# Turning q and k by VectorE 32x32 transposes, with four-tile scores, a list schedule and shared PSUM banks

## The chip, the cores and the metric

The kernel runs on one core of one Trainium2 chip. The metric is device time in microseconds (us) of one execution. A run over 1.5% above the fastest of the same kernel is called slow and takes no part in a ratio. TensorE is called PE, its weight loads PEld, VectorE DVE, ScalarE ACT, GpSimd POOL, as in the profile.

## The reference, cut to what matters

Attention with a window of 128 keys and four sink keys, in 4 batches of 8 heads, followed by an MLP mixer on each batch.

```python
B, H, S, D = 4, 8, 768, 64            # q, k, v = randn * 0.1; n_sink 4, window 128
keep = is_sink | ((rel >= 0) & (rel < window))
a = softmax(where(keep, q @ k.T / 8, -1e9))
x = (a @ v) -> [4, 768, 512]
h = relu(x.T @ w_tok1) @ w_tok2       # w_tok1 [768, 256]
u = x + h.T
out = u + relu(u @ w_ch1) @ w_ch2     # w_ch1 [512, 1536], out float32
```

The two channel matmuls are called ch1 and ch2 below, the token matmuls tok1 and tok2. In the profile ch1 writes the tile `ps_v`, ch2 `ps_w`, tok1 `ps_h`, tok2 `ps_u`, the scores `ps_s`, probabilities times v `ps_o`. A group is four heads, so there are eight groups, g0 to g7, two for each batch.

## The kernel before

q and k come with token in the partition, and the score matmuls of this kernel read them with the head dimension there. Heads go in pairs: six PE transposes turn 2 heads x 768 tokens of q or k into PSUM, a VectorE copy takes the result out to bf16, and a score matmul contracts over 64 rows, two heads side by side.

```python
def load_qk(eng, src, dst, G, lo, hi):
    return eng.dma_start(out=dst[:, lo:hi].rearrange("p h t d -> p h (t d)"),
        in_=src[G.b, G.h0 + lo:G.h0 + hi].rearrange("h (p t) d -> p h (t d)", t=NT))
# ... (cut)
def tr(j, which):                       # j: pair of heads, which: q or k
    src = G.qb if which == 0 else G.kb
    ps = ps_ms.tile([P, NT, P], BF16, name="ps_tr", tag="ms")
    for t in range(NT):                 # NT = 6
        nc.tensor.transpose(ps[:, t], src[:, j, t].rearrange("p i d -> p (i d)"), ident)
    dst = att.tile([P, S], BF16, name="qT" if which == 0 else "kT")
    (by_act if g == 0 and j == 0 and which else by_dve)(
        dst.rearrange("d (p t) -> d p t", t=NT), ps.rearrange("d t p -> d p t"))
# ... (cut) scores of one pair:
    for kt, w in kts:
        for i in range(2):
            nc.tensor.matmul(ps[:, i, at:at + w],
                G.kT[j][ds(64 * i, 64), ts(kt, P)], G.qT[j][ds(64 * i, 64), ds(kt * P, w)], ...)
```

The copy out writes its destination without gaps and reads PSUM with a step. The order of instructions is made by hand: the attention of the next batch is spread between the mixer's matmuls by fractions. PSUM has two two-bank score tiles, two banks for the mixer (`mx`) and two for the rest (`ms`).

The softmax here doesn't subtract the row's maximum and nothing guards it: scores larger than these inputs give would overflow.

Of the kernel before, what the change touches and what calls it, by code (L numbers as in the profile page):

```python
# [12 lines left out]
ALU = mybir.AluOpType  # L13


@with_exitstack
def kernel(
# [13 lines left out]
    nc = tc.nc  # L31
# [12 lines left out]
    HS = S // 2  # L44
    D1 = D + 1
    scale = 1.0 / float(D) ** 0.5

    singles = ctx.enter_context(tc.tile_pool(name="singles", bufs=1))
    stage = ctx.enter_context(tc.tile_pool(name="stage", bufs=2))
    bfp = ctx.enter_context(tc.tile_pool(name="bfp", bufs=2))  # L50
    att = ctx.enter_context(tc.tile_pool(name="att", bufs=3))
    ptp = ctx.enter_context(tc.tile_pool(name="ptp", bufs=4))
    small = ctx.enter_context(tc.tile_pool(name="small", bufs=4))
    xpool = ctx.enter_context(tc.tile_pool(name="xpool", bufs=2))
    mix = ctx.enter_context(tc.tile_pool(name="mix", bufs=2))
    osb = ctx.enter_context(tc.tile_pool(name="osb", bufs=4))
    ps_sc = ctx.enter_context(tc.tile_pool(name="ps_sc", bufs=2, space=bass.MemoryType.PSUM))
    ps_mx = ctx.enter_context(tc.tile_pool(name="ps_mx", bufs=2, space=bass.MemoryType.PSUM))
    ps_ms = ctx.enter_context(tc.tile_pool(name="ps_ms", bufs=2, space=bass.MemoryType.PSUM))

    ident = singles.tile([P, P], BF16, name="ident")
    mask0 = singles.tile([P, 2, 2, P], BF16, name="mask0")
    mneg = singles.tile([P, 2, 2, 2, P], BF16, name="mneg")
    warm = singles.tile([P, 512], BF16, name="warm")
    ks = [[singles.tile([P, P], BF16, name=f"ks{a}{j}") for j in range(2)] for a in range(2)]
    vs_f = singles.tile([4 * GH, NG, GH, D1], FP32, name="vs_f")
    vsink = singles.tile([P, NG, GH, D1], BF16, name="vsink")

# [5 lines left out]
    SYNC = mybir.DependencyInfo(mybir.DependencyClass.Sync, mybir.DependencyReason.DATA)  # L74

    def after(dma, *others):
        for o in others:
            tc.add_manual_dep(dma.ins, o.ins.name, SYNC, reason="order of loads")
        return dma
# [4 lines left out]
    def tiles(g):  # L84
        G = Group()
        G.b, G.h0 = g // GB, GH * (g % GB)
        G.q32 = stage.tile([P, GH, NT, D], FP32, name="q32")
        G.k32 = stage.tile([P, GH, NT, D], FP32, name="k32")
        G.qb = bfp.tile([P, 2, NT, 2, D], BF16, name="qb")
        G.kb = bfp.tile([P, 2, NT, 2, D], BF16, name="kb")  # L90
        G.v32 = stage.tile([P, GH, NT, D], FP32, name="v32")
        G.va = bfp.tile([P, GH, NT, D1], BF16, name="va")
        G.qT, G.kT, G.pT = [None, None], [None, None], [None, None]
        return G


    def load_qk(eng, src, dst, G, lo, hi):
        return eng.dma_start(
            out=dst[:, lo:hi].rearrange("p h t d -> p h (t d)"),
            in_=src[G.b, G.h0 + lo:G.h0 + hi].rearrange("h (p t) d -> p h (t d)", t=NT))  # L100

    def load_q(G, lo, hi, eng=nc.sync):
        return load_qk(eng, q, G.q32, G, lo, hi)

    def load_k(G, lo, hi, eng=nc.sync):
        return load_qk(eng, k, G.k32, G, lo, hi)

    def cast(G, j, which, copy):
        src, dst = ((G.q32, G.qb), (G.k32, G.kb))[which]
        copy(dst[:, j].rearrange("p t i d -> p i t d"), src[:, 2 * j:2 * j + 2])  # L110

    def by_dve(o, i):
        nc.vector.tensor_copy(out=o, in_=i)  # L113

    def by_pool(o, i):
        nc.gpsimd.tensor_copy(out=o, in_=i)

    def by_act(o, i):
        nc.scalar.activation(o, i, AF.Copy)

    def load_v(G):
        return nc.sync.dma_start(out=G.v32.rearrange("p h t d -> p (h t) d"),
                                 in_=v[G.b, G.h0:G.h0 + GH].rearrange("h (t p) d -> p (h t) d", p=P))

    def load_sinks():
        for h in range(GH):
            nc.sync.dma_start(
                out=vs_f[4 * h:4 * h + 4, :, h, 0:D],
                in_=v.rearrange("b (a h) s d -> h s (b a) d", h=GH)[h, 0:4])

    def load_tok():
        nc.gpsimd.dma_start(out=w_tok1, in_=moe_w_tok1.rearrange("(t p) n -> p t n", p=P))
        nc.gpsimd.dma_start(out=w_tok2, in_=moe_w_tok2.rearrange("(t p) n -> p t n", p=P))

    def load_ch1(i):
        hf = DCH // 2
        return nc.gpsimd.dma_start(out=w_ch1[:, :, ts(i, hf)],
                            in_=moe_w_ch1.rearrange("(t p) n -> p t n", p=P)[:, :, ts(i, hf)])

    def load_ch2(i):  # L140
        hf = NF // 2
        nc.gpsimd.dma_start(out=w_ch2[:, ts(i, hf)],
                            in_=moe_w_ch2.rearrange("(t p) n -> p t n", p=P)[:, ts(i, hf)])

    def build_masks():

        z = mneg.rearrange("p m x c q -> p (m x) c q")
        nc.gpsimd.affine_select(
            out=z[:, :, 0], in_=z[:, :, 0], compare_op=ALU.is_ge,
            fill=-30000.0, base=0, pattern=[[0, 4], [1, P]], channel_multiplier=-1)  # L150
        nc.gpsimd.affine_select(
            out=z[:, :, 1], in_=z[:, :, 1], compare_op=ALU.is_ge,
            fill=-30000.0, base=-1, pattern=[[0, 4], [-1, P]], channel_multiplier=1)
        nc.vector.memset(mneg[0:4, 0, 0], 0.0)

    def build_mask0():
        nc.vector.memset(mask0, 1.0)
        nc.gpsimd.affine_select(
            out=mask0[:, :, 0], in_=mask0[:, :, 0], compare_op=ALU.is_ge,
            fill=0.0, base=0, pattern=[[0, 2], [1, P]], channel_multiplier=-1)  # L160
        nc.gpsimd.affine_select(
            out=mask0[:, :, 1], in_=mask0[:, :, 1], compare_op=ALU.is_ge,
            fill=0.0, base=-1, pattern=[[0, 2], [-1, P]], channel_multiplier=1)
        nc.vector.memset(mask0[0:4], 1.0)

    def build_sinks():

        one = vs_f[:, :, :, D]
        nc.gpsimd.memset(one, 1.0)
        nc.gpsimd.affine_select(  # L170
            out=one, in_=one, compare_op=ALU.is_ge, fill=0.0,
            base=0, pattern=[[0, NG], [-4, GH]], channel_multiplier=1)
        nc.gpsimd.affine_select(
            out=one, in_=one, compare_op=ALU.is_ge, fill=0.0,
            base=3, pattern=[[0, NG], [4, GH]], channel_multiplier=-1)

    def cast_sinks():
        nc.vector.tensor_copy(out=vsink[0:4 * GH], in_=vs_f)

    def cast_v(G):  # L180
        nc.gpsimd.memset(G.va[:, :, :, D:D1], 1.0)
        nc.gpsimd.tensor_copy(out=G.va[:, :, :, 0:D], in_=G.v32)


    def attention(g, G, x_b, first):
        c0 = GH * D * (g % GB)
        kz = ks[g % 2]

        def tr(j, which):
            src = G.qb if which == 0 else G.kb  # L190
            ps = ps_ms.tile([P, NT, P], BF16, name="ps_tr", tag="ms")
            for t in range(NT):
                nc.tensor.transpose(ps[:, t], src[:, j, t].rearrange("p i d -> p (i d)"), ident)  # L193
            dst = att.tile([P, S], BF16, name="qT" if which == 0 else "kT")
            (by_act if g == 0 and j == 0 and which else by_dve)(
                dst.rearrange("d (p t) -> d p t", t=NT), ps.rearrange("d t p -> d p t"))
            if which == 0:
                G.qT[j] = dst
            else:
                G.kT[j] = dst  # L200
                for i in range(2):
                    nc.vector.tensor_copy(out=kz[j][ds(64 * i, 64), ds(8 * j + 4 * i, 4)],
                                          in_=ps[ds(64 * i, 64), 0:4, 0])

        def sc(j, u):
            if u == 0:
                G.pT[j] = ptp.tile([P, 2, 12 * P], BF16, name="pT")
            ps = ps_sc.tile([P, 2, 512], FP32, name="ps_s", tag="sc")
            kts = [(kt, (2 if kt < NT - 1 else 1) * P) for kt in (2 * u, 2 * u + 1)]
            n = sum(w for _, w in kts)  # L210
            if first:
                for i in range(2):
                    nc.tensor.matmul(ps[:, i, 0:n], ident,
                                     mneg[:, min(u, 1)].rearrange("p x c q -> p (x c q)")[:, 0:n],
                                     start=True, stop=False, skip_group_check=True)
            at = 0
            for kt, w in kts:
                for i in range(2):
                    nc.tensor.matmul(  # L219
                        ps[:, i, at:at + w],  # L220
                        G.kT[j][ds(64 * i, 64), ts(kt, P)], G.qT[j][ds(64 * i, 64), ds(kt * P, w)],
                        start=not first, stop=not first or at > 0, skip_group_check=first)
# [266 lines left out]
```

## Time and profile before

| | before |
|---|---|
| median of 3 runs | 239.03 us (238.72 to 239.09) |
| span of the profiled run | 237.1 us |
| busy: PE, DVE, ACT, POOL | 212.1, 100.6, 114.1, 88.9 us |
| first ch1 matmul starts | 36.6 us |
| from there to the end | 200.5 us |

From the page of the kernel before: busy time by engine, the granted TensorE clock in 40 slices of the span (9 is 90% or more of full speed), the chain of waits that ended last by engine, and the group of copies that empty the PE transposes (busy us, mean ns of one, then idle time before it).

```profile
PE 212.1 (89%) x1708; PEld 119.8 (51%) x1729; DVE 100.6 (42%) x221; ACT 114.1 (48%) x195; POOL 88.9 (37%) x124
...
PEclk9999999999999999999999999999999999999999
...
PE 68%; POOL 10%; DVE 9%; ACT 6%; DMA 3%; issue 2%; ACTq 0%; POOLq 0%
...
L113 DVE COPY qT<-ps_tr 128x768 bf16<-128x768 bf16 x16 | 15.3, 957 | 35.2 <-PE ps_tr L193 35.0
```

PE is busy 89% of the span, at full clock throughout, and holds 68% of the chain. VectorE is at 42%.

From the view of waits, PE's own, kernel before: who waited for whom, us in total, times, longest.

```profile
PE ps_tr L193 <- POOL qb L116: 4.6, 3, 1.8
PE ps_s L219 <- ACT pT L225: 3.1, 6, 1.0
```

No wait of PE is long: the largest kind adds up to 4.6 us in the whole run.

### The profile page before, as it was taken

How to read it: one execution, taken by the hardware profiler on the slowest of the kernel's cores; microseconds unless marked ns; L12 is line 12 of the kernel's file. 1: busy time of each engine (PE TensorE's matmuls, PEld its weight loads, DVE VectorE, ACT ScalarE, POOL GpSimd, SP SyncE). 2: the span in 40 equal slices, each digit the busy share in tenths (PEclk: the TensorE clock that was granted, in tenths of full speed). 3: DMA queues.
4: the chain of work that ended last, by engine and by line, in shares of the span. 5: the costliest groups of instructions: out<-in, count | busy, mean ns of one | idle time of the engine just before them, and what ended most of it. 6: DMA issues, size and time to landing. Idle time of an engine off the chain costs nothing.

```text
span 237.1 us, 4195 instructions
## 1 busy us (share of the span) xinstructions
PE 212.1 (89%) x1708; PEld 119.8 (51%) x1729; DVE 100.6 (42%) x221; ACT 114.1 (48%) x195; POOL 88.9 (37%) x124
## 2 busy tenths in 40 slices
PE   6797788976999999978999999978999999999993
PEld 2334545552556544645566445635566445554441
DVE  5687663070845454707526334707526334001131
ACT  2585536759472123595772233695762133653300
POOL 3567400449989200079985000089950000000000
PEclk9999999999999999999999999999999999999999
DMA  6999999999994111893911021100001021101122
GB/s 215 303 258 144 206 189 258 283 327 248 267 328 109 72 44 44 240 205 90 304 54 44 0 91 46 44 0 3 13 34 44 14 78 44 46 3 44 44 88 88
DMA packets 40659, 29.40 MB, mean 124 GB/s; under 512 B 25664, under 2 KB 37696, under 8 KB 40640
## 3 DMA queue, kind: packets, MB, share of 16 engines
q1 hardware_dynamic: 36000, 23.89, 36.8%
q0 software_dynamic: 3680, 3.93, 10.1%
q10 hardware_dynamic: 960, 1.31, 1.6%
q8 instruction: 13, 0.21, 0.4%
q14 instruction: 6, 0.05, 0.1%
HBM read 26.77 MB, written 6.29 MB: 139 GB/s over the span
## 4 chain that ended last, share of the span: by engine, by line
PE 68%; POOL 10%; DVE 9%; ACT 6%; DMA 3%; issue 2%; ACTq 0%; POOLq 0%
PE ps_w L313 26%; PE ps_v L304 20%; DVE o L316 5%; ACT pT L225 5%; PE ps_h L285 3%; PE ps_tr L193 3%; PE ps_u L292 3%; DMA k_113<-in_k_dram 3%; PE ps_s L219 3%; POOL pT L236 2%; PE ps_ut L298 2%; PE ps_o L257 2%; PE ps_o L253 2%; DVE x_b L265 2%; POOL pT L239 2%
## 5 line engine op out<-in xcount | busy, mean ns | idle before, releaser
L304 PE MATMUL ps_v<-uT,w_ch_103 128*128 128x384 bf16 x384 | 74.3, 325 | 1.4 <-ACT uT L299 0.7
L304 PEld LDWEIGHTS <-w_ch_103 128*128 128x128 bf16 x384 | 34.7, 97 | 25.0 <-issue 6.8
L225 ACT ACTIVATE pT<-ps_s 128x1024 bf16<-128x1024 f32 (+1 forms) x48 | 43.6, 961 | 7.1 <-PE ps_s L219 6.9
L229 POOL TENSOR_TENSOR pT<-pT,mask_92 128x512 bf16<-128x512 bf16 x12 | 13.8, 1154 | 52.2 <-ACT pT L225 52.2
L316 DVE TENSOR_TENSOR o<-ps_w,u_sb 128x512 f32<-128x512 f32 x24 | 16.6, 692 | 39.5 <-PE ps_w L313 39.5
L113 DVE COPY qT<-ps_tr 128x768 bf16<-128x768 bf16 x16 | 15.3, 957 | 35.2 <-PE ps_tr L193 35.0
L299 ACT ACTIVATE uT<-ps_ut 128x512 bf16<-128x512 bf16 x24 | 14.0, 596 | 32.6 <-PE ps_ut L298 32.5
L293 DVE TENSOR_TENSOR u_sb<-ps_u,x_b 128x512 bf16<-128x512 f32 x24 | 16.4, 689 | 25.9 <-PE ps_u L292 25.9
L265 DVE TENSOR_TENSOR x_b<-ps_o,rc 128x256 bf16<-128x256 f32 x48 | 20.4, 424 | 1.7
L236 POOL TENSOR_SCALAR_AFFINE_SELECT pT<-pT 128x640 bf16<-128x640 bf16 x24 | 18.0, 752 | 5.5 <-ACT pT L225 5.5
L219 PE MATMUL ps_s<-qT,kT 64*128 64x256 bf16 x192 | 15.5, 263 | 4.6 <-ACT pT L225 3.1
L264 DVE RECIPROCAL rc<-ps_o 128x4 f32<-128x4 f32 x48 | 8.5, 178 | 25.9 <-PE ps_o L261 13.1
L313 PE MATMUL ps_w<-w_ch_104,v_581 128*128 128x512 bf16 x69 | 18.1, 379 | 0.8 <-DVE o L316 0.6
L313 PE MATMUL ps_w<-w_ch_104,v_1338 128*128 128x512 bf16 x69 | 18.1, 379 | 0.8 <-DVE o L316 0.6
L313 PE MATMUL ps_w<-w_ch_104,v_111 128*128 128x512 bf16 x67 | 17.9, 379 | 0.8 <-DVE o L316 0.3
L306 ACT ACTIVATE v_1338<-ps_v 128x384 bf16<-128x384 f32 x24 | 11.9, 506 | 12.5 <-PE ps_v L304 12.5
L306 ACT ACTIVATE v_581<-ps_v 128x384 bf16<-128x384 f32 x24 | 11.9, 506 | 12.6 <-PE ps_v L304 12.6
L257 PE MATMUL ps_o<-va,pT 128*128 128x65 bf16 x192 | 17.3, 194 | 0.2
L306 ACT ACTIVATE v_2035<-ps_v 128x384 bf16<-128x384 f32 x24 | 11.8, 491 | 11.3 <-PE ps_v L304 11.2
L257 PEld LDWEIGHTS <-pT 128*128 128x128 bf16 x192 | 14.5, 98 | 3.5 <-issue 0.4
L306 ACT ACTIVATE v_111<-ps_v 128x384 bf16<-128x384 f32 x24 | 11.8, 495 | 9.0 <-PE ps_v L304 8.8
L313 PE MATMUL ps_w<-w_ch_104,v_2035 128*128 128x512 bf16 x70 | 15.9, 379 | 0.1
(102 smaller groups left out, 280.2 us busy)
## 6 DMA issues: line engine op xcount, KB each, us to landing
out_dram<-o SPq DMA_DIRECT2D x23, 256.0 KB, 2.0
w_ch_103<-in_moe_w_ch_dram POOLq DMA_DIRECT2D x2, 768.0 KB, 9.4
w_ch_104<-in_moe_w_ch_dram POOLq DMA_DIRECT2D x2, 768.0 KB, 13.8
k_113<-in_k_dram ACTq DMA_DIRECT2D x2, 384.0 KB
q_112<-in_q_dram SPq DMA_DIRECT2D x2, 384.0 KB, 5.8
q_118<-in_q_dram SPq DMA_DIRECT2D x2, 384.0 KB, 5.5
v_116<-in_v_dram SPq DMA_DIRECT2D x1, 768.0 KB, 10.9
v_122<-in_v_dram SPq DMA_DIRECT2D x1, 768.0 KB, 7.2
```

Source lines behind the costliest of these rows:

```text
L113: nc.vector.tensor_copy(out=o, in_=i)
L219: nc.tensor.matmul(ps[:, i, at:at + w], G.kT[j][ds(64 * i, 64), ts(kt, P)], G.qT[j][ds(64 * i, 64), ds(kt * P, w)], start=not first, stop= ...
L225: nc.scalar.activation(pT[:, :, 512 * u:512 * u + n], ps[:, :, 0:n], AF.Exp, scale=scale)
L236: nc.gpsimd.affine_select(out=cur, in_=cur, compare_op=ALU.is_ge, fill=0.0, base=0, pattern=[[0, NT - 1], [1, P]], channel_multiplier=-1)
L257: nc.tensor.matmul(ps[:, h], pT[:, i, ds(256 * qt, P)], G.va[:, h, qt], start=(qt < 2 and h == 0), stop=(h == GH - 1 and qt == 0), skip_gr ...
L265: nc.vector.tensor_tensor(out=x_b[:, qt, c0:c0 + GH * D].rearrange("p (h d) -> p h d", h=GH), in0=ps[:, :, 0:D], in1=rc.to_broadcast([P, G ...
L293: nc.vector.tensor_tensor(out=u_sb[:, st], in0=ps, in1=x_b[:, st], op=ALU.add)
L299: nc.scalar.activation(uT[:, :, ts(st, P)], ps, AF.Copy)
L304: nc.tensor.matmul(ps, w_ch1[:, c, ts(ft, P)], uT[:, c, ds(half * HS, HS)], start=(c == 0), stop=(c == NC - 1))
L306: nc.scalar.activation(v1[:, ft, ds(half * HS, HS)], ps, AF.Relu)
L313: nc.tensor.matmul(ps, v1[:, ft, ts(st, P)], w_ch2[:, ft], start=(ft == 0), stop=(ft == NF - 1))
L316: nc.vector.tensor_tensor(out=o, in0=ps, in1=u_sb[:, st], op=ALU.add)
```

## The change

The intent is to take the q and k transposes off PE and out of PSUM. q and k are loaded so that partition 32h+i holds 24 consecutive tokens of head h. VectorE then transposes 32x32 blocks, each holding 32 tokens by 32 of the 64 head dimensions, straight from SBUF to SBUF. Scores contract over 32 rows in two passes (`db`), four heads on four row tiles. The instruction order now comes from a list scheduler that simulates each engine with assumed durations. Additive mask matmuls stay for g0 only. All single-bank PSUM tiles share four banks. The core of the diff, with cuts marked:

```diff
-    return eng.dma_start(
-        out=dst[:, lo:hi].rearrange("p h t d -> p h (t d)"),
-        in_=src[G.b, G.h0 + lo:G.h0 + hi].rearrange("h (p t) d -> p h (t d)", t=NT))
+    nc.sync.dma_start(out=t, in_=heads(src, g).rearrange("h (i r) d -> (h i) (r d)", i=Q))      # Q = 32
@@ transposes @@
-    for t in range(NT):
-        nc.tensor.transpose(ps[:, t], src[:, j, t].rearrange("p i d -> p (i d)"), ident)
-    ... copy ps_tr to qT / kT on DVE
+    nc.vector.transpose(
+        G.T[w][:, db, ds(hf * n, n)].rearrange("p (i r) -> p r i", i=Q),
+        G.bf[w][:, hf].rearrange("p (r x j) -> p x r j", x=DB, j=Q)[:, db])
+    return op(f"T{w}{g}.{hf}{db}", ("DVE", dve(rr * Q) - 0.09), emit, [c] + old, base)
@@ scores @@
+    for kt, w in nk:
+        for db in range(DB):                                     # DB = 2
+            for h in hs:
+                nc.tensor.matmul(bank[h][:, at:at + w], G.T["k"][r, db, ts(kt, P)],
+                                 G.T["q"][r, db, ds(kt * P, w)], ..., tile_position=(Q * h, 0))
@@ PSUM @@
-    ps_sc, ps_mx, ps_ms: pools of two
+    slots = {"sc": 2, "mx": 4}
@@ order @@
-    run(spread(main, fill))            # hand-made fractions
+    for o in order_of(ops, slots):     # list schedule
+        o.emit(o.engine)
... (cut: about a thousand lines, most of them the same work written as operations)
```

Token 24i+r has to land in column 24i+r, so the transpose's output is written `"p (i r) -> p r i"`. And the scheduler believes that one 128x768 transpose takes `dve(768) - 0.09`, which is 0.87 us.

## The prediction

> **What bounds the kernel now.** TensorE. The page's busy table gives PE 212.1 of 237.1 us (89%), ACT 48%, DVE 42%, POOL 37%; in the chain of waits PE holds 68%. Granted clock 1.00. In the timeline four ch1 matmuls (384 columns) take 0.65 us, four ch2 matmuls (512) 0.86 us. Three stages: start to the first ch1 matmul at 36.6 us; three mixers overlapped with the next batch's attention (58.3, 53.0, 53.1 us from ch1 to ch1); the last mixer and tail, 36.1 us.
>
> In a 53.0 us stage I add up starts read from the timeline: ch1 and ch2 31.1, tok1 and tok2 5.2, u transposes 1.35, scores 3.0, sink scores and P·V 4.3, q/k transposes 2.7 (six per 0.335 us). That is 47.6; 5.4 us are lost, 3.3 of them visible as PE idle (waits table: score matmuls behind the exponential, transposes behind POOL's cast, up to 1.8 us each)[...].
>
> **What the change does.**
> 1. Removes 192 PE transposes: 192 x 0.056 = 10.7 us of PE, all but about 2.7 us on the critical path. Removes 31 PSUM copies on DVE (0.955 us) and 32 small ones (0.155): 34.5 us. Adds 32-row-block transposes on DVE, equal to 32 of 128x768; estimated from that copy at 0.9 us: 29 us. DVE also takes masks and evictions, but stays below 65%: hidden. [...]
> 2. Scores: K=64 pairs become two K=32 passes over four tiles, so the same column time. Before: 8 matmuls in 0.49 us. After: 16 in 0.45 to 0.6 us. Gain about 0. [...]
> 3. Group 1's additive mask matmuls go: 2 us of PE, early.
> 4. Order and four mixer banks instead of two: should recover about half of the 3.3 us idle per stage, and more in the 58.3 us one: 6 to 9 us.
> 5. Start: less sure. The order listing shows eight k loads on ACT's queue, the later four waiting for the first, ahead of the ACT table load (1.28 us) and ACT's k cast, so the first exponential comes near 10.5 us (8.25 before); group 2's q, k, v loads no longer wait for the ch1 weights, and compete with v and weights (DMA is saturated, 0.95 to 1.17, in the first 60 us). I expect the first ch1 matmul at 33 to 37 us.
>
> **Sum.** PE work after: about 181 us, 14 before the first ch1. 34.5 + 167 + stalls and drains 9 + tail 4 = 214.5 us span, plus 1.9 (239.0 against 237.1) = 216 us; range 208 to 225. Faster by over 2%: 0.95; within 2%: 0.04; slower: 0.01.
>
> **Right or wrong.** PE busy should fall to about 190-195 us with no ps_tr group; DVE's transposes read 0.8 to 0.95 us; ch1-to-ch1 stages 47 to 50 us; waits of PE on ACT exponentials and POOL casts shrink; score groups of 16 at 0.45 to 0.6 us; tail unchanged.
>
> **What would make it wrong.** DVE transposes far over 0.95 us (strided writes); four-tile scores not concurrent (about 1.7 us each 16, +25 us); v or ch1 weights landing late, so the start grows past 40 us; the in-order schedule stalling where real times differ from its assumed ones.

The sum came to 214.5 us of span (34.5 + 167 + 9 + 4). Those 9 us were the author's estimate. What the trace of the kernel before shows is about 0.10 us at a score group: from their first start to the next group's first, four ch1 matmuls take 0.75 us when a score group follows and 0.65 us when PE transposes follow. The "about 1.7 us" of the last paragraph is an estimate as well: sixteen matmuls of 256 columns one after another at the rate of the ch1 ones, 0.65 us for four of 384. The DMA share called saturated reads 0.84 in the first 10 us and 1.06 to 1.17 in the five windows of 10 us after them.

## The result and the profile after

| | before | after |
|---|---|---|
| median | 239.06 us (238.72 to 240.07, 4 runs) | 302.01 us (301.17 to 302.69, 4 runs) |
| span profiled | 237.1 us | 300.1 us |
| first ch1 | 36.6 us | 63.2 us |
| first ch1 to the end | 200.5 us | 236.9 us |

The ratio is 1.262, with a 95% interval of 1.257 to 1.267. Ratios here are the mean time of one kernel's fast runs over that of the other's fast runs of the same rounds, so not quite the ratio of the medians quoted. The changed kernel is 26% slower, where 10% faster was predicted.

From the page of the kernel after: busy time, VectorE's busy tenths, granted clock, and the chain by engine and by line.

```profile
PE 225.8 (75%) x1734; PEld 121.1 (40%) x1734; DVE 211.5 (70%) x254; ACT 104.4 (35%) x171; POOL 73.2 (24%) x95
...
DVE  6999959589889959998977996893258852110112
...
PEclk9655557699999779759758799795999999999999
...
DVE 48%; PE 44%; DMA 5%; issue 1%; ACT 1%; ACTq 0%; SPq 0%; DVEq 0%
DVE kT L356 19%; PE ps_w L618 17%; DVE qT L356 16%; PE ps_v L596 13%; DMA raw_k<-in_k_dram 5%; DVE pT L437 4%; DVE x_b L515 3%; PE ps_s L406 3%; PE ps_h L539 3%; PE ps_u L559 3%; PE ps_ut L575 2%; PE ps_k L476 1%; DVE u_sb L566 1%; DVE o L628 1%; DVE rc L514 1%
```

VectorE went from 100.6 to 211.5 busy us and now holds 48% of the chain; in that chain the transposes alone (line 356) are 35% of the span. Its busy digits stand near 9 for the first two thirds. The PE clock is no longer at full speed (0.846 in the mean, against 1.00).

The groups with shapes kept apart, kernel after, line 356:

```profile
L356 DVE STREAM_TRANSPOSE kT<-kb 128x768 bf16<-128x768 bf16 x14 | 51.8, 3837 | 0.0
L356 DVE STREAM_TRANSPOSE qT<-qb 128x768 bf16<-128x768 bf16 x14 | 51.3, 3718 | 0.0
L356 DVE STREAM_TRANSPOSE kT<-kb 128x384 bf16<-128x384 bf16 x4 | 7.4, 2032 | 0.0
L356 DVE STREAM_TRANSPOSE qT<-qb 128x384 bf16<-128x384 bf16 x4 | 7.2, 1880 | 0.0
```

One 128x768 transpose takes 3.7 to 3.8 us, not 0.9. Together they take 118 us (the four lines added), where 29 us were predicted. The waits view shows the consequence on PE, to be set against the 4.6 and 3.1 us shown of before:

```profile
PE ps_s L406 <- DVE kT L356: 26.1, 8, 6.2
PE ps_ut L575 <- DVE u_sb L566: 6.9, 2, 4.8
PE ps_o L491 <- DVE x_b L515: 6.7, 3, 5.1
```

Score matmuls wait for the turned k. The second and third lines each end with a short VectorE instruction (an addition of 0.7 us, an eviction of 0.4 us), yet PE waits up to 5 us for it. What stood before it on VectorE is not the same in both. The longest wait of each, from the timelines (start us, us; first the third line, then the second):

```profile
47.61 5.16 DVE L437 TENSOR_TENSOR pT<-pT,mrest 128x512 bf16<-128x512 bf16 x2
47.20 2.42 POOL L674 DMA_DIRECT2D w_ch<-in_moe_w_ch_dram  x3
53.39 0.40 PE L491 MATMUL ps_o<-vsink,pk 128*128 128x260 bf16 x1 [5.11 <-DVE x_b L515]
...
124.74 7.21 DVE L356 STREAM_TRANSPOSE kT<-kb 128x768 bf16<-128x768 bf16 x2
132.82 0.61 PE L575 MATMUL ps_ut<-ident,u_sb 128*128 128x128 bf16 x4 [4.85 <-DVE u_sb L566]
```

The wait of 4.85 us is for an addition that stands behind two transposes of k (7.21 us). The wait of 5.11 us has no transpose before it: two mask multiplies span 5.16 us, one of them 4334 ns, while POOL goes through load issues and into its casts. That is a second trouble, which sections 7 and 8 take up.

One step that could have been blamed is innocent. The timeline of PE, kernel after, in a stretch at full clock (start us, us, then engine, line, operation):

```profile
219.24 0.62 PE L406 MATMUL ps_s<-qT,kT 32*128 32x256 bf16 x16
219.79 1.04 PE L476 MATMUL ps_k<-qT,kz 128*128 128x512 bf16 x4
```

From the first start to the next there are 0.55 us for 16 matmuls on four row tiles. That is inside the predicted 0.45 to 0.6 us, and far from the estimated 1.7 us of sixteen one after another.

### The profile page after: what moved, and what is told of

Same layout as the page of the kernel before. It is cut to its first block, busy times and chain, and to the rows that moved or that the text cites. A ratio compares the mean times of both kernels' runs of the same rounds, so it can differ in the third digit from the quotient of the medians.

```text
span 300.1 us, 4228 instructions
## 1 busy us (share of the span) xinstructions
PE 225.8 (75%) x1734; PEld 121.1 (40%) x1734; DVE 211.5 (70%) x254; ACT 104.4 (35%) x171; POOL 73.2 (24%) x95
## 4 chain that ended last, share of the span: by engine, by line
DVE 48%; PE 44%; DMA 5%; issue 1%; ACT 1%; ACTq 0%; SPq 0%; DVEq 0%
DVE kT L356 19%; PE ps_w L618 17%; DVE qT L356 16%; PE ps_v L596 13%; DMA raw_k<-in_k_dram 5%; DVE pT L437 4%; DVE x_b L515 3%; PE ps_s L406 3%; PE ps_h L539 3%; PE ps_u L559 3%; PE ps_ut L575 2%; PE ps_k L476 1%; DVE u_sb L566 1%; DVE o L628 1%; DVE rc L514 1%
## 5 line engine op out<-in xcount | busy, mean ns | idle before, releaser
L596 PE MATMUL ps_v<-uT,w_ch 128*128 128x384 bf16 x384 | 72.3, 338 | 7.7 <-DVE o L628 4.6
L618 PE MATMUL ps_w<-w_ch,v 128*128 128x512 bf16 (+1 forms) x300 | 70.7, 388 | 0.0
L356 DVE STREAM_TRANSPOSE kT<-kb 128x768 bf16<-128x768 bf16 (+1 forms) x18 | 59.3, 3436 | 0.0
L356 DVE STREAM_TRANSPOSE qT<-qb 128x768 bf16<-128x768 bf16 (+1 forms) x18 | 58.5, 3310 | 0.1
L197 ACT ACTIVATE v<-ps_v 128x384 bf16<-128x384 f32 x79 | 38.7, 492 | 55.5 <-PE ps_v L596 44.4
L204 POOL TENSOR_SCALAR_AFFINE_SELECT pT<-pT 128x512 bf16<-128x512 bf16 x27 | 19.3, 723 | 142.5 <-ACT pT L423 138.5
L596 PEld LDWEIGHTS <-w_ch 128*128 128x128 bf16 x384 | 36.9, 100 | 34.8 <-issue 9.5
L406 PE MATMUL ps_s<-qT,kT 32*128 32x256 bf16 (+1 forms) x384 | 23.7, 314 | 27.7 <-DVE kT L356 26.1
L618 PEld LDWEIGHTS <-v 128*128 128x128 bf16 x300 | 29.8, 102 | 32.4 <-issue 6.0
L406 PEld LDWEIGHTS <-kT 32*128 32x128 bf16 x384 | 11.3, 105 | 43.5 <-DVE kT L356 28.7
L494 PE MATMUL ps_o<-va,pT 128*128 128x65 bf16 x192 | 18.4, 208 | 8.6 <-DVE pT L444 4.3
L491 PE MATMUL ps_o<-vsink,pk 128*128 128x260 bf16 x32 | 10.0, 312 | 10.9 <-DVE x_b L515 6.7
L499 PE MATMUL ps_o<-va,pT 128*128 128x65 bf16 x160 | 17.0, 207 | 0.0
## 6 DMA issues: line engine op xcount, KB each, us to landing
w_ch<-in_moe_w_ch_dram POOLq DMA_DIRECT2D x1, 1024.0 KB, 11.2
```

What stands on the lines that cost most here:

```text
L197: nc.scalar.activation(o, i, AF.Relu)
L204: eng.affine_select(out=t, in_=t, compare_op=ALU.is_ge, fill=fill, base=0, pattern=[[0, t.shape[1]], [1, P]], channel_multiplier=-1)
L356: nc.vector.transpose(G.T[w][:, db, ds(hf * n, n)].rearrange("p (i r) -> p r i", i=Q), G.bf[w][:, hf].rearrange("p (r x j) -> p x r j", x= ...
L406: nc.tensor.matmul(bank[h][:, at:at + w], G.T["k"][r, db, ts(kt, P)], G.T["q"][r, db, ds(kt * P, w)], start=not first and db == 0, stop=db ...
L494: nc.tensor.matmul(ps[:, h], G.pT[qt // 2][:, h, ds(256 * (qt % 2), P)], G.va[:, h, qt], start=(qt < 2 and h == 0), stop=(h == GH - 1 and ...
L596: nc.tensor.matmul(ps, w_ch1[:, c, ts(ft, P)], M.uT[hf][:, c], start=(c == 0), stop=(c == NC - 1))
```

## The experiments

The theory after the result was: the step of the transposes' output makes them slow, and that is most of the loss. The rivals were a cost of the transpose itself or of its stepped input, a stalled schedule whatever the transposes cost, the four-tile scores, and, for the start of the run, the loads or the clock. Thirteen kernels ran. Ratios are to the kernel before, run in the same batch on the same chip; its median there was 238.7 to 239.1 us.

### 1. The disputed cost by itself (p1_costs)

A bench instead of the kernel: each form of the instruction four times on an otherwise free VectorE, zeros stored as output, so its result is wrong on purpose (one run, its state unknown). ScalarE and GpSimd did some copies of the same kind meanwhile. Its core:

```diff
+ dense = src[:, 0:N].rearrange("p (r j) -> p r j", j=32)
+ nc.vector.transpose(flat.rearrange("p (r i) -> p r i", i=32), dense)           # L59: no step
+ nc.vector.transpose(packed.rearrange("p (r i) -> p r i", i=32), half)          # L61: gaps in the input only
+ nc.vector.transpose(w24.rearrange("p (i r) -> p r i", i=32), dense)            # L63: writes 24 apart
+ ... the same with 12, 8, 4, 2 (L65, L67, L69, L71) and for float32 (L73 none, L75 24, L77 4, L79 2)
+ nc.vector.tensor_copy(out=c24.rearrange("p (i r) -> p r i", i=32), in_=dense)  # L81: copy, writes 24 apart
+ nc.vector.tensor_copy(out=cr24..., in_=src[:, 0:N].rearrange("p (r i) -> p i r", i=32))  # L83: copy, reads 32 apart
```

> A bench of single instructions, its result wrong on purpose (zeros). Each form of 128x768 runs four times in a row on an idle engine. Theory W (the write step of 24 elements makes the transpose slow): bf16 written densely 0.85 to 0.95 us, whether the source is dense or has 64-element rows; written at a step of 24 about 3.7 us; steps 2, 4, 8, 12 in between, rising once the step passes a few elements. Theory T (the transpose itself is slow on 2-byte data): all forms about 3.7 us. Theory B (contention with GpSimd and other engines in the full kernel): the step of 24 is near 0.9 us here, where nothing else runs. Plain copies with the same write step tell whether only the transpose pays. Score groups of 16 matmuls: 0.45 to 0.6 us, and the same with operands read at a step of 2 elements if that is free.

Groups of the bench on VectorE, shapes kept apart (busy us, mean ns of one):

```profile
L63 DVE STREAM_TRANSPOSE w<-src 128x768 bf16<-128x768 bf16 x4 | 15.0, 3742 | 0.1
L67 DVE STREAM_TRANSPOSE w<-src 128x768 bf16<-128x768 bf16 x4 | 14.5, 3618 | 0.1
...
L75 DVE STREAM_TRANSPOSE f_w<-src 128x768 f32<-128x768 f32 x4 | 8.3, 2075 | 0.1
L69 DVE STREAM_TRANSPOSE w<-src 128x768 bf16<-128x768 bf16 x4 | 7.7, 1922 | 0.1
L81 DVE COPY c<-src 128x768 bf16<-128x768 bf16 x4 | 7.7, 1918 | 0.1
...
L71 DVE STREAM_TRANSPOSE w<-src 128x768 bf16<-128x768 bf16 x4 | 4.1, 1027 | 0.1
L61 DVE STREAM_TRANSPOSE packed<-src 128x768 bf16<-128x768 bf16 x4 | 3.9, 968 | 0.1
...
L59 DVE STREAM_TRANSPOSE flat<-src 128x768 bf16<-128x768 bf16 x4 | 3.9, 965 | 0.1
L83 DVE COPY cr<-src 128x768 bf16<-128x768 bf16 x4 | 3.3, 827 | 0.1
```

The transpose takes 965 ns when it writes densely, the same with a gapped input, and 3742 ns with the change's step of 24. Step 2 is nearly free (1027), step 4 doubles it (1922), step 8 is already the full price (3618). So it is the step of the write; neither a transpose as such (965) nor gaps in its input (968) is slow. Nor is it GpSimd: its last copy ended 23.6 us into the run, and step 8 ran from 43 us on. A plain copy shows the same side: 1918 ns if it writes 24 apart, 827 if it reads 32 apart. The bench has no dense copy, so what that read step costs a copy is not known; and the same write step costs a transpose about twice what it costs a copy, for which no run shows a reason. As 4-byte words the step of 24 costs 2075 ns, and 768 columns of words are 1536 bf16 elements, so turned in words the price of an element falls from 4.87 ns (3742 / 768) to 1.35 ns (2075 / 1536).

### 2. The same kernel with dense writes (e1_dense)

One edit to the changed kernel. Columns of qT and kT come out permuted, so scores and values no longer belong together: wrong. (The chip's comparison still passed it: with inputs this small the scores are near zero and the softmax near uniform. The author saw the error in a numerical check off the chip, with q and k scaled by 20; that check is not on record.)

```diff
-                    G.T[w][:, db, ds(hf * n, n)].rearrange("p (i r) -> p r i", i=Q),
+                    G.T[w][:, db, ds(hf * n, n)].rearrange("p (r i) -> p r i", i=Q),
```

> The changed kernel with one thing undone: the transposes write their blocks densely, not at a step of 24 elements; the columns then stand in another order, so the result is wrong on purpose, while every other instruction and its order stays. Theory W: a transpose falls from 3.7 to about 0.9 us, DVE busy from 211 to about 115 us, granted clock back to 1.00, time 205 to 222 us. Theory T or B: a transpose stays at 3.7 us and the time at 302 us.

Measured: 230.98 us, ratio 0.9675 (0.963 to 0.972). From its page and its groups by shape:

```profile
PE 206.1 (90%) x1716; PEld 116.3 (51%) x1734; DVE 129.4 (56%) x254; ACT 104.3 (45%) x171; POOL 73.4 (32%) x95
...
PEclk9955557799999999999999999999999999999999
...
PE 70%; DVE 16%; issue 8%; POOL 4%; ACT 0%; POOLq 0%
```

```profile
L356 DVE STREAM_TRANSPOSE qT<-qb 128x768 bf16<-128x768 bf16 x14 | 13.3, 964 | 0.0
L356 DVE STREAM_TRANSPOSE kT<-kb 128x768 bf16<-128x768 bf16 x14 | 12.8, 945 | 0.0
```

With the order of instructions and every declared wait the same, dense writes give 71 us back (302.01 - 230.98). This settles the main cause: the step of the write, 71 of the 86 us by which the prediction missed. The transposes fell as theory W said; its 205 to 222 us and its full clock (0.94 measured) did not come. Not all of the 71 us are transposes that PE waits for. With the slow ones PE also ran at a lower granted clock, 0.846 against 0.94, and its busy time was 19.7 us longer for the same matmuls (225.8 against 206.1; e1's trace lacks 18 records), and the longest mask multiply took 4334 ns against 1683. The remaining 15 us are in the start: the first ch1 begins at 47.8 us instead of the predicted 33 to 37. From there to the end it is 181.4 us, where the prediction's sum had 180 (167 + 9 + 4).

### 3. The slow transpose, but a schedule that knows it (e2_costed)

```diff
-            return op(f"T{w}{g}.{hf}{db}", ("DVE", dve(rr * Q) - 0.09), emit, [c] + old, base)
+            return op(f"T{w}{g}.{hf}{db}", ("DVE", 4.75e-3 * rr * Q + 0.13), emit, [c] + old, base)
```

> The changed kernel with its list schedule told the measured cost of a transpose (3.78 us for 768 columns in place of 0.87); nothing else. It moves about 24 optional operations (masks, evictions) off DVE and orders the rest anew; the transposes stay as slow. Rival theory S (the transposes would fit; the in-order schedule built on a wrong duration stalls): 215 to 235 us. Theory D (VectorE's own work is the bound): DVE busy about 195 us, time 240 to 280 us.

Measured: 253.85 us, ratio 1.057 (1.049 to 1.065). The transposes take what they took (118 us: 59.1 and 59.0 for q and k on its page), yet 48 of the 71 us are gone. The profiled run was slow, 255.5 us, so no finer reading is taken from it. The time lies in the range of theory D, as does VectorE's busy time (191.3 us in that profile, 195 foretold); theory S's 215 to 235 us were not reached. So the same slow instruction cost 71 us in a schedule that believed 0.87 us for it, and some 23 us (253.85 - 230.98) in one that knew. The two kernels differ in their whole order, and VectorE has 221 instructions instead of 254, so this is a comparison of schedules: what the order brought and what the work taken off VectorE is not separated. Both follow from the one wrong duration.

### 4. The start: do the early weight loads hold up v? (s1_v_first)

In the dense variant the first v landed 20 us after its issue (10.9 in the kernel before), with weight loads on the wire at the same time. This edit makes the first weight load wait on the landing of v of g0 and g1, on top of e1 (wrong values again).

```diff
+            for G in groups[:2]:
+                tc.add_manual_dep(dma.ins, G.vdma.ins.name, SYNC, reason="order of loads")
-    weight("tok1", ..., [v1st])
+    weight("tok1", ..., [v1st, groups[1].load["v"]])
```

> The kernel with dense transposes (result wrong on purpose) with one thing added: the weight loads of the GpSimd queue wait until v of groups 0 and 1 has landed. Theory V (the first ch1 matmul at 47.8 us there is late because v, in 256-byte rows, shares the DMA engines with the weights and lands 20 us after its issue): v lands within 12 us of its issue, the first P.V starts before 22 us, first ch1 at 36 to 41 us, time 220 to 226 us. Rival theory C (the half clock of 11 to 37 us and the exponentials behind it set the start): first ch1 stays within 3 us of 47.8 and the time at 228 to 233 us. Rival theory Q (all loads are needed anyway, so holding the weights only moves the wait to them): v early, but first ch1 waits for weights at 45 us or later.

Measured: 235.91 us, ratio 0.985 (0.981 to 0.989), one of four runs slow at 256.5 us and, by ill luck, the profiled one. 5 us slower than e1, outside the times of theories V and C. In the slow profile both v landed within 11.2 us of their issue, as theory V wanted, but PE then waited 7.4 us for the load of w_tok1, and the first ch1 came at 54.9 us: the wait had moved to the weights, as theory Q said, as far as a slow run can tell. The order of the loads alone did not help in this form.

### 5. Correct values at a smaller price (w1_words, w1s_words_v_first)

The bench suggests a kernel that is right: turn pairs of bf16 as 4-byte words. The word transpose still writes 24 apart, at 2.1 us for all 64 dimensions in place of two of 3.7. The two halves of a pair come out in neighbouring columns and the score matmuls read them at step 2; the bench had a score group of 16 at 0.57 us that way, against 0.55. The second kernel also places the weight loads, in the schedule, behind the cast of the second v.

```diff
-                    G.T[w] = att.tile([P, DB, S], BF16, name=w + "T")
+                    G.T[w] = att.tile([P, S, DB], BF16, name=w + "T")
-                    G.T[w][:, db, ds(hf * n, n)].rearrange("p (i r) -> p r i", i=Q),
-                    G.bf[w][:, hf].rearrange("p (r x j) -> p x r j", x=DB, j=Q)[:, db])
+                    G.T[w].rearrange("p s x -> p (s x)").bitcast(FP32)[:, ds(hf * n, n)].rearrange("p (i r) -> p r i", i=Q),
+                    G.bf[w][:, hf].bitcast(FP32).rearrange("p (r j) -> p r j", j=Q))
-                            nc.tensor.matmul(bank[h][:, at:at + w], G.T["k"][r, db, ts(kt, P)],
+                            nc.tensor.matmul(bank[h][:, at:at + w], G.T["k"][r, ts(kt, P), db],
... (cut: the other reads of G.T likewise, one transpose in place of two, its assumed duration 2.6e-3 * rr * Q + 0.1)
@@ w1s_words_v_first only @@
+    for w in w_ops.values():
+        w.deps.append(groups[1].cv)
```

> A right version with the loads as they are: two bf16 of one row are turned as one 4-byte word, so half as many elements go through the transpose; the write step stays at 24 elements, now of 4 bytes. Sixteen transposes of 768 words at 2.08 us (the bench) in place of 32 of 3.7 us: 33 us of DVE instead of 118. The score matmuls read at a step of two elements (the bench: 0.57 against 0.55 us for 16). Time 228 to 235 us, like the dense one; if it stays above 245 us, write cost is not what counts.

> The word version, with the weight loads placed behind the cast of the second v in the GpSimd queue (the schedule is made anew with that). Theory V: first ch1 at 36 to 42 us, time 219 to 226 us, faster than the kernel before by 5% or more. Theory C or Q: no better than the word version without it.

Measured: 229.62 us, ratio 0.959 (0.955 to 0.963), first ch1 at 50.3 us; and 225.35 us, ratio 0.941 (0.938 to 0.945), first ch1 at 42.0 us. All runs fast, results correct on the chip (and, by the author, with q and k scaled by 20 off the chip, which is not on record). Both are inside their expected ranges. Groups by shape of the second:

```profile
L356 DVE STREAM_TRANSPOSE kT<-kb 128x768 f32<-128x768 f32 x7 | 14.7, 2100 | 0.0
L356 DVE STREAM_TRANSPOSE qT<-qb 128x768 f32<-128x768 f32 x7 | 14.5, 2076 | 0.0
```

Its chain is 82% PE. Later in the schedule, and not behind a hard wait as in s1, the weights cost v nothing: v landed at most 11.3 us after its issue (20.7 in w1), and the first ch1 came 8.3 us sooner than in w1. But the loads are not all of that. In w1 PE waits 3.40 us for the cast of v, and later longer still:

```profile
41.72 0.40 PE L491 MATMUL ps_o<-vsink,pk 128*128 128x260 bf16 x1 [5.45 <-DVE x_b L515]
```

Before that wait three mask multiplies span 5.78 us on VectorE, the longest 3084 ns, under POOL's load issues and casts (section 7); in w1s PE waits 0.61 us at that point. So the early v and the luckier meeting of the two engines came in one edit, and no run tells their shares. This version beats both kernels.

### 6. A cheaper write step bought with smaller loads (w2s_words_rows2)

As w1s, with q and k loaded in 512-byte pieces so that the words stand two apart, at the price of four DMAs a tensor instead of one.

```diff
-                nc.sync.dma_start(out=t, in_=heads(src, g).rearrange("h (i r) d -> (h i) (r d)", i=Q))
+                for h in range(GH):
+                    nc.sync.dma_start(out=t[Q * h:Q * h + Q].rearrange("i (c x) -> i c x", x=2 * D),
+                                      in_=heads(src, g)[h].rearrange("(c i e) d -> i c (e d)", i=Q, e=2))
... (cut: g0's loads likewise, the transposes' output, the assumed durations)
```

> As the last, with q and k loaded so that a partition holds pairs of rows (512-byte pieces, four DMAs a tensor), which makes the word transposes write at a step of two words: 0.97 us in place of 2.08 (the bench), 18 us of DVE less. If DVE time is still on the critical path: 3 to 8 us faster than the last. If PE bounds it: the same within 1%. If the smaller pieces slow the loads at the start: slower.

Measured: 237.45 us, ratio 0.993 (0.988 to 0.997). The transposes took 970 ns, as the bench said, and VectorE is down to 111.3 busy us from 121.1, but the first ch1 comes at 51.1 us instead of 42.0. This is the third branch of the expectation. That the loads are what lost is likely and not shown: the schedule was made anew, and 4.2 us of the loss come after the first ch1 (185.8 us from there to the end, against 181.6).

### 7. Clock, number of loads, and banks (x1 to x4)

All four start from w1s. There PE has a gap of 3.2 us before its first score, and it runs at half clock from about 9 to 33 us: the clock read 0.50 from 10 to 20 us, though PE was busy 9.38 of those 10 us.

```diff
@@ x1_long_warm (and x3_both) @@
-        for _ in range(14):
+        for _ in range(23):                       # warm-up matmuls
-    op("dummy", ("PE", 5.0), dummy, [o_warm], -300)
+    op("dummy", ("PE", 8.8), dummy, [o_warm], -300)      # the scheduler is told, and makes the order anew
@@ x2_few_loads (and x3_both): the halves of g0's q and k by one DMA each, not one a head @@
-                for h in range(GH):
-                        eng.dma_start(out=G.raw[w][Q * h:Q * h + Q, hf],
-                                      in_=src[0, h, ds(hf * HS, HS)].rearrange("(i r) d -> i (r d)", i=Q))
+                    eng.dma_start(out=G.raw[w][:, hf],
+                                  in_=src[0, 0:GH, ds(hf * HS, HS)].rearrange("h (i r) d -> h i (r d)", i=Q))
@@ x4_split_banks @@
-    slots = {"sc": 2, "mx": 4}
+    slots = {"sc": 2, "mx": 2, "ms": 2}
```

> The word-transposing kernel with the weights held (225.35 us), with one edit: 23 warm-up matmuls instead of 14, so that TensorE has no gap between the end of the warm-up (7.05 us) and the first score (10.28 us). Theory C (the half clock from 10 to 31 us is the price of that 3.2 us gap): the clock between 10 and 30 us is 0.9 to 1.0 instead of 0.50, a score group of 8 takes about 0.5 instead of 1.03 us, and the first ch1 starts 2 to 5 us sooner than 42.0 us, 221 to 223 us in all. Rival D (the start waits for the loads of v and the weights, and TensorE's clock there costs nothing): the clock may rise, but the first ch1 stays within 1 us of 42 us and the time within 1 us of 225. Rival F (the sparse work of this stretch lowers the clock whatever came before): the clock is 0.50 again soon after 10 us.

> The same base kernel (225.35 us), one edit: the first group's half tensors of q and k are loaded by one DMA each (4 in all) instead of one a head (16), so that the queue gets to the first v load sooner: its issue should come at 2.5 to 4 us instead of 8.4. Theory D: v then lands some 4 us sooner, and the first ch1 starts 2 to 4 us sooner than 42.0; 222 to 224 us. Rival C (the clock binds this stretch): v lands sooner, the first ch1 moves by less than 1 us, 224.5 to 226 us. If fewer and larger DMAs land later, the first score comes later than 10.3 us and both are lost.

> Both edits on the same base. If both causes are real and add up: first ch1 at 35 to 38 us, 219 to 221 us. If only one of them binds: the time of the better of the two single runs.

> The same base kernel (225.35 us), one edit: the four shared PSUM banks are split two and two again, one pair for scores of the sink, P V and the u transposes, one for the mixer's sums, as in the kernel before; the schedule is recomputed for it. Theory (the shared banks are worth 2 to 4 us of the stages after the start, as the prediction's step 4 had them): 227 to 230 us, with first ch1 near 42 us and a longer remainder. Rival (with the list order, nothing waits for a bank): 225 to 226 us.

| | median us | ratio to before | first ch1, us |
|---|---|---|---|
| w1s (base) | 225.35 | 0.941 | 42.0 |
| x1, long warm-up | 232.65 | 0.974 | 48.9 |
| x2, few loads | 245.84 | 1.026 | 56.1 |
| x3, both | 239.84 | 1.003 | 55.9 |
| x4, banks split | 235.01 | 0.982 | 46.5 |

All four are misses in the sense that no expectation held its number. The few loads were far worse: PE did nothing between 10 and 20 us, the DMA engines were 26% busy at 95 GB/s between 16 and 28 us, and the first v landed 26.1 us after its issue. Why so little moved there, no run shows. The split banks cost 9.7 us; in the profiled runs it is 10.9 us, 4.5 of them before the first ch1 and 6.4 after it (188.0 us from there to the end, against 181.6). The expectation gave the banks 2 to 4 us. The schedule was recomputed, so this is the worth of four shared banks under this scheduler.

The long warm-up did keep the clock full up to 12 us. Then it fell again, after a gap of 1.0 us (another, of 1.4 us, had ended 1.7 us before it), as rival F had it: at 31.8 us P·V matmuls still started 0.055 us apart, against 0.03 us from 32.6 us on. But that is not where 7 us went. VectorE and POOL in the timeline of x1 (start us, us):

```profile
32.23 6.57 DVE L437 TENSOR_TENSOR pT<-pT,mrest 128x512 bf16<-128x512 bf16 x2
32.60 0.69 POOL L204 TENSOR_SCALAR_AFFINE_SELECT pT<-pT 128x512 bf16<-128x512 bf16 x1
33.20 2.44 POOL L674 DMA_DIRECT2D w_ch<-in_moe_w_ch_dram  x3
35.58 1.53 POOL L192 CAST qb<-raw_q 128x1536 bf16<-128x1536 f32 x1
36.99 1.53 POOL L192 CAST kb<-raw_k 128x1536 bf16<-128x1536 f32 x1
...
39.41 0.40 PE L491 MATMUL ps_o<-vsink,pk 128*128 128x260 bf16 x1 [6.47 <-DVE x_b L515]
```

Two mask multiplies span 6.57 us on VectorE while POOL goes without a pause through three load issues and into its casts, and PE waits 6.47 us for what stands behind them. The durations of those multiplies (ns: least, median, most) from the view of that line:

```profile
L437 DVE TENSOR_TENSOR pT<-pT,mrest x14: 415/476/4139, 25.9 to 162.0; 128x512 bf16<-128x512 bf16 x14
```

One of them took 4139 ns instead of some 420, the other 2510. Both ran while POOL worked, and section 8 tests whether that is the cause. How POOL holds a multiply is not shown, and whether it is its load issues, its casts or its mask select, no run separates; the one of 2510 ns (32.23 to 34.74) ran under a mask select and load issues alone. The same is seen in the changed kernel (4334 ns), in w1 (3084 ns), and smaller in e1, where two such multiplies span 3.19 us under three load issues.

### 8. The collision taken away (x7_warm_yield, x8_yield)

The order of the instructions stays that of x1 (x7) or of w1s (x8). POOL's weight loads and casts of the start now wait for the multiplies that VectorE has been given before them.

```diff
+    def behind_masks(i):
+        m = getattr(groups[1], "on_dve", None)
+        if m is not None and len(waited) < 12:
+            waited.append(i)
+            tc.add_manual_dep(i.ins, m.ins.name, SYNC, ...)
+        return i
-               "POOL": lambda o, i: nc.gpsimd.tensor_copy(out=o, in_=i),
+               "POOL": lambda o, i: behind_masks(nc.gpsimd.tensor_copy(out=o, in_=i)),
-            nc.gpsimd.dma_start(out=dst, in_=src)
+            behind_masks(nc.gpsimd.dma_start(out=dst, in_=src))
```

> The long-warm-up kernel (232.65 us, first ch1 at 48.9) with one more edit that leaves the order of the instructions alone: GpSimd's weight loads and casts of the start wait until VectorE's mask multiplies of the second group are done. In that kernel one such multiply took 4139 ns instead of 417, while GpSimd went from three load issues into two casts, and TensorE sat idle for 6.5 us (32.8 to 39.4). Theory G (VectorE's multiply of two SBUF tensors was held off by GpSimd, and that is where the 7 us of the long warm-up went): the longest multiply is under 1.1 us, the first ch1 comes at 41 to 43.5 us, 224 to 227 us in all. Rival H (the longer multiply is a symptom: TensorE's second fall to half clock is the loss): the time stays at 231 to 234 us whatever the multiply takes.

> The same edit on the base (225.35 us, first ch1 at 42.0), where the longest multiply took 1025 ns. Theory G: at most 1 us is to be had, 224 to 226 us. A larger gain would say that the wait also helps something else[...].

Measured: x7 225.28 us, ratio 0.942 (0.939 to 0.946), first ch1 at 40.9 us; x8 225.05 us, ratio 0.942 (0.938 to 0.946), first ch1 at 41.8 us. The same view for x7, where the line has become 448, over the start:

```profile
L448 DVE TENSOR_TENSOR pT<-pT,mrest x7: 416/420/852, 24.8 to 31.5; 128x512 bf16<-128x512 bf16 x7
```

The longest multiply is 852 ns and the 7 us of x1 are back, by letting POOL wait 0.8 us. So the loss of x1 was the collision of POOL with VectorE's masks, and the rival, that the second fall of the clock was the loss, falls. x8 gains nothing that can be told from w1s, as expected; the edit did not shorten its longest multiply (1364 ns, against 1025 in w1s).

The two together also say something of what the clock is worth. Windows of x7, then of x8 (busy us of PE, PEld, DVE, ACT and POOL, granted clock, DMA share, GB/s):

```profile
10.00:20.00 10.00, 8.71 (x57) 3.11 (x62) 8.15 (x10) 6.27 (x7) 1.45 (x1) 0.62 1.22 278
20.00:30.00 10.00, 7.85 (x116) 5.57 (x107) 5.19 (x16) 5.98 (x8) 5.63 (x9) 0.70 0.99 255
30.00:40.00 10.00, 8.25 (x90) 5.59 (x88) 7.63 (x23) 3.33 (x7) 8.81 (x10) 1.00 1.26 193
```

```profile
10.00:20.00 10.00, 9.31 (x59) 3.33 (x60) 7.65 (x9) 6.10 (x7) 1.05 (x1) 0.57 1.12 275
20.00:30.00 10.00, 8.34 (x101) 5.56 (x98) 6.28 (x18) 5.88 (x7) 5.72 (x9) 0.50 0.98 256
30.00:40.00 10.00, 8.34 (x91) 6.12 (x89) 7.34 (x20) 2.94 (x6) 8.76 (x10) 0.91 1.23 185
```

x7 has the better clock in every window and begins ch1 0.9 us sooner, and the total is the same. That prices only the part of the clock that x7 won back: over these 30 us its mean is 0.77 against 0.66, and the kernel before had 1.00 there. What the full clock would bring, no run shows, and it may be more: up to the first ch1 PE is busy 33.34 of 40.9 us in x7 at a clock of 0.83, and 27.95 of 36.6 us in the kernel before at 1.00, so x7 loses nothing there by idling (7.6 us against 8.7). The DMA share, near or above 1 in both, fits a stretch that waits for loads, but no run took the loads away.

## Why the prediction was wrong, point by point

The predicted sum was 214.5 us of span, the measured span 300.1.

1. **"Adds 32-row-block transposes on DVE … estimated from that copy at 0.9 us: 29 us"** is the step that failed. They took 3.7 to 3.8 us each and 118 us in all. The reference was wrong: the copy at 957 ns writes densely and has its step on the read side, the transpose writes 24 elements apart. p1 shows 965 ns dense and 3742 ns at that step, e1 shows 71 us of the kernel's time hanging on it. The risk was named ("DVE transposes far over 0.95 us (strided writes)") and given almost no weight: the chance of slower stood at 0.01. With it fell "stays below 65%: hidden", as VectorE read 70%.
2. **The start, "I expect the first ch1 matmul at 33 to 37 us"**, failed too, by a smaller amount. With dense transposes it is 47.8 us (e1). Holding the weight loads back in the schedule brought 8.3 us between w1 and w1s, some of it by a smaller collision of POOL with the masks, and x7 came to 40.9. The prediction named late v and weights as a risk, and v did land late (20 us in e1). It did not think of POOL holding up VectorE's masks (4139 ns for one of some 420 in x1), nor of the half clock (0.50 in w1s). The last 4 to 5 us against the 36.6 of the kernel before are not explained by any run: about 1.6 us of them are tok2 matmuls and u transposes that the new order does before the first ch1, and the lower clock is a candidate that was not tested to the end.
3. **"The in-order schedule stalling where real times differ from its assumed ones"** was named as a risk and was true in size: of the 71 us about 48 went away when only the assumed duration was mended (e2), by a new order and by less work on VectorE together.
4. **Scores: "16 in 0.45 to 0.6 us"** held: 0.55 us. Against the estimated 1.7 us one after another, the four tiles do run at the same time.
5. **From the first ch1 on**, the sum of 180 us held once the writes were dense: 181.4 us in e1, 181.6 in w1s, against 200.5 before. So the gain of about 19 us that the change was made for is real, but for the 1.6 us of work moved into the start; it comes from PE transposes, order and banks together. In e1's trace PE is busy 13.3 us less there than before (170.8 against 184.2) and idle 5.8 us less. The parts fit less well than the sum, so some of that fit is luck: the stages from ch1 to ch1 took 52.0, 49.9 and 45.0 us in e1 where 47 to 50 each was said, and the tail, said to be unchanged, 34.5 us (37.1 before by the same count, which the prediction read as 36.1). Only the banks were told apart (x4, about 6 us after the first ch1). What the mask matmuls of g1 brought, and what changes between kinds of matmul cost, was not tested.
6. **"PE busy should fall to about 190-195 us"** was off even with the cause removed: 206.1 us in e1. Part of that is matmuls at the lower clock of the start (0.59 from 10 to 20 us, 0.50 from 20 to 30): from start to start, two mask matmuls took 0.53 us at 10.9 us and 0.97 us at 14.1 us. The rest was not taken apart.

## What to carry to other kernels

Cost an instruction from one with the same access pattern on its output, not only with the same shape: on VectorE a bf16 write that steps by 8, 12 or 24 elements made a transpose 3.7 to 3.9 times as long, while gaps in its input cost nothing (968 against 965 ns). When a layout forces such a step, move elements in 4-byte words (1.35 against 4.87 ns for a bf16 element in the bench) and let the next reader take the step, if a run shows that it reads nearly for free (here 0.57 against 0.55 us for 16 score matmuls). A list schedule is only as good as its durations and the one here knew nothing of POOL holding up VectorE (4139 ns for a multiply of some 420), so check its assumed times against the first profile before judging the idea, and look behind a short instruction that PE waits for: the time may belong to what stood before it.
